# Attention ahead of two MoE layers: the maxima of the first six head pairs move to another PSUM pool

## The chip, the cores and the metric

The kernel runs on one core of one Trainium2 chip. The metric is the device time of one execution in microseconds (us). Before the change three runs took 1105.35, 1109.31 and 1111.76 us; the median is 1109.31 us.

## What is computed

Attention over 4 batches, 12 heads, 448 positions and 64 channels, then two MoE-like layers on 1792 tokens of width 768. Cut to what matters:

```python
q_n, k_n = rmsnorm(q, g_q), rmsnorm(k, g_k)
scores = scale * q_n @ k_n.T
scores = scores - max(scores, axis=-1)          # a maximum per query
attn = exp(scores); attn /= sum(attn) + 1e-9
x = (attn @ v)            # laid out as (1792, 768)
h = x @ w_in1; sm = softmax(h); x = layernorm(h * sm) * g_ln @ w_out1     # 768 -> 1024 -> 768
h = x @ w_in2; out = (h - tanh(h)) @ w_out2                               # 768 -> 2048 -> 768
```

The weights arrive as 64-bit floats and are converted on the chip; a product is made of three matmuls of a high and a low part (`three`, L189).

## The kernel before

**Pairs.** Two heads of one batch make a pair: 24 pairs, six to a batch (`HP = 6`). For a pair `p` the steps are:

- `load_qk`, `norm`: load and normalise q and k.
- `qk_trans` (L272): two **turns**, of k and of q. TensorE transposes into a PSUM tile `qkps`; ScalarE takes the high part and VectorE the low part, and DMAs copy both into the large tiles `K` and `Q` (`k<-wk`, `q<-wq`).
- `maxima` (L333): seven matmuls of 128 queries by 448 keys (`mps`); VectorE reduces each to a column of `nm` (L351, 0.6 us). The scores are only wanted for their maxima here.
- `spread` (L353): for each head `n` of the pair (`n = 2p`, `2p + 1`), `nm` is transposed (`nmps`), ScalarE writes the row `nt`, and a DMA of 2 KB puts it into a row of `Q` (`q<-nt`, L363). So the score matmuls subtract the maximum by themselves.
- `weights` (L365): the scores the other way round, in tiles `sps` of 128 keys by 448 queries, three to a head and one for the tails of both. A tile takes two matmuls: the first (z = 0) doesn't need the row of maxima, the second (z = 1) does (in pair 0: three, L380 to L382, and the fourth, L383). ScalarE makes the exponential `pf` (L395).
- `pv` (L399): `pf` times v into `pvps`; `pv_fin` and `x_norm` divide and store.

**PSUM.** Eight banks in three pools (L678 to L680): `ps_m` with three banks for the turns, the spread and the first MoE layer; `ps_x` with three for the maxima and for the scores; `ps_v` with two for `pvps`. Within a pool the tiles take the banks in turn, in the order of the program text: the fourth tile waits until the first has been read.

**Order.** The steps are written into a list with a slot (a head) and a step in it (a quarter of a slot), L452 to L476; the maxima of head `n` stand in slot `n`, its scores about two slots later. A scheduler then places the instructions of each engine's queue anew, by when operands and buffers come free in its own estimate; what stands below as the order is its result. The slots up to 15 are written ahead of everything else (L719): attention alone. They hold the maxima of pairs 0 to 7. After that `overlap` (L722) weaves the rest of the attention into the stages of the first MoE layer, whose first matmul is the first `hps` (L190). The second layer (`h2ps`, `ops`) comes last and fills TensorE alone.

**Streams.** While the first pairs run, the conversion of the first layer's weights has begun: loads of 512 KB (`raw<-in_moe_w_in_dram`, L115), work on ScalarE, VectorE and GpSimd (L135 to L161), and stores of 512 KB (`w_in<-w`, L164). All DMAs but three are issued from SP's queue, in its order.

Of the kernel before, what the change touches and what calls it, by code (L numbers as in the profile page):

```python
# [8 lines left out]
F32 = mybir.dt.float32  # L9
# [9 lines left out]
def kernel(  # L19
# [15 lines left out]
    B, H, S, D = q.shape  # L35
# [6 lines left out]
    HP = H // 2  # L42
# [169 lines left out]
    def qcols(t, o, p, i, z):  # L212

        c = (2 + i) * S + GAP if p == 0 else QO[i, z]
        return t[o, c:c + S]
# [117 lines left out]
    def maxima(p, c):  # L333


        if p not in nm_t:
            nm_t[p] = A["small"].tile([128, 7], F32, tag="nm", name="nm")
        ps = ps_x.tile([128, S], F32, tag="x", name="mps")
        i = c // 4
        r = slice(64 * i, 64 * i + 64)  # L340
        if c == 3:
            nc.tensor.matmul(ps, lhsT=qd[p % 2], rhs=w_t[p, 1][:, 0], start=True, stop=True)
        else:
            if p == 0:
                qh, kh = Q[0][r, 0:S], w_t[0, 1][r, 0]
            else:

                qh, kh = qcols(Q[p % NQ], slice(0, 128), p, i, 0), K[p % NQ][:, i, 0]
            f = 128 * c if i == 0 else 128 * (c - 4) + 64
            nc.tensor.matmul(ps, lhsT=qh[:, f:f + 128], rhs=kh, start=True, stop=True)  # L350
        nc.vector.tensor_reduce(out=nm_t[p][:, c:c + 1], in_=ps, axis=AX.X, op=ALU.max, negate=True)  # L351
# [100 lines left out]
    for p in range(NP):  # L452
        s = 2 * p
        at(s - 7, 0, load_qk, p)
        if 1 <= p <= NQ:
            at(s - 2 if p < NQ else 4, 1, fill, p % NQ)
            at(s - 2 if p < NQ else 4, 1, fill_q, p % NQ)
        at(s, 1, load_v, p)
        at(s - 3, 1, norm, p)
        at(s - 2, 2, qk_trans, p, 1)  # L460
        at(s - 1, 0, qk_trans, p, 0)
        for i in range(2):
            n, z = s + i, 4 * (s + i)
            for j, c in enumerate((3, 0, 1, 2) if i == 0 else (4, 5, 6)):
                step(z + j, maxima, p, c)
            step(z + 4, spread, n)
            for j in range(3):
                step(z + LAG + j, weights, n, j)
                step(z + LAG + 4 + j, pv, n, j)
        step(z + LAG + 3, weights, s + 1, 3)  # L470
        step(z + LAG + 4, pv_tails, s)
        step(z + LAG + 4, pv_fin, s)
        step(z + LAG + 6, pv_fin, s + 1)
        step(z + LAG + 8, x_norm, p)
# [203 lines left out]
    ps_m = ctx.enter_context(tc.tile_pool(name="ps_m", bufs=3, space=PSUM))  # L678
    ps_x = ep.enter_context(tc.tile_pool(name="ps_x", bufs=3, space=PSUM))
# [199 lines left out]
```

## Time and profile before

| | |
|---|---|
| median of three runs (lowest, highest) | 1109.31 us (1105.35, 1111.76) |
| span of the profiled execution, which is the time that the page gives of it | 1107.5 us |
| TensorE matmul busy | 1043.3 us, 94% |
| VectorE, ScalarE, GpSimd busy | 690.5, 493.1 and 236.4 us |
| first matmul; first matmul of an MoE layer (`hps`) | 11.28 us; 127.04 us |

A busy matmul row reaches from its start to its modelled end, so rows overlap, and a row that follows a slower one looks longer than its share of the engine. What one instruction takes from the engine is better read from the chain of waits, where each piece ends where the next begins.

### The profile page before, as it was taken

The page shows a single profiled execution, that of the slowest core. Times are in us where ns is not written, and L with a number is a line of the kernel's source. Part 1 is how long each engine was busy: PE and PEld are TensorE (multiplying, and loading weights), DVE is VectorE, ACT ScalarE, POOL GpSimd, SP SyncE. Part 2 cuts the span into 40 slices and gives each one's busy share as a digit, 9 for nine tenths or more (in the row PEclk, how much of TensorE's full clock was granted, in tenths as well). Part 3 has the DMA queues.
Part 4 walks back from the last instruction along what each step waited for, and adds up shares of the span by engine and source line. Part 5 has one row for each costly group of instructions (what it writes and reads, how often), then busy time and mean ns, then how long its engine had stood idle before and what let it go on. Part 6 is the DMA issues. An engine that isn't in the chain of part 4 may idle for free.

```text
span 1107.5 us, 15169 instructions
## 1 busy us (share of the span) xinstructions
PE 1043.3 (94%) x5348; PEld 864.2 (78%) x5348; DVE 690.5 (62%) x1311; ACT 493.1 (45%) x994; POOL 236.4 (21%) x204
## 2 busy tenths in 40 slices
PE   4989999989887899999999999999999999999998
PEld 2555566648664678778889989898999989898988
DVE  8766686787787453633684066475767666675444
ACT  4667776777677455555255154311212121212110
POOL 2511123121102110001420034242414141322000
PEclk9999999989988999999999999999999999999999
DMA  7987789866996987666786443021112111110004
GB/s 182 274 227 192 179 216 281 207 181 178 284 320 185 327 229 216 192 209 203 227 291 208 138 162 95 23 74 39 57 40 59 55 58 58 57 57 1 1 29 171
DMA packets 113743, 171.16 MB, mean 155 GB/s; under 512 B 31940, under 2 KB 79492, under 8 KB 113668
## 3 DMA queue, kind: packets, MB, share of 16 engines
q1 hardware_dynamic: 112368, 170.20, 52.8%
q8 instruction: 42, 0.69, 0.3%
q14 instruction: 33, 0.27, 0.1%
q10 hardware_dynamic: 1300, 0.01, 0.1%
HBM read 109.32 MB, written 29.10 MB: 125 GB/s over the span
## 4 chain that ended last, share of the span: by engine, by line
PE 72%; DMA 15%; DVE 6%; ACT 4%; issue 1%; SPq 1%; POOL 1%; ACTq 0%; DVEq 0%; POOLq 0%
PE pvps L409 9%; PE ops L191 7%; PE ops L192 7%; PE ops L190 7%; PE h2ps L191 7%; PE h2ps L192 7%; PE h2ps L190 7%; PE sps L386 4%; DMA raw<-in_moe_w_out_dram 3%; PE x2ps L190 3%; PE x2ps L191 3%; PE x2ps L192 3%; DMA q<-nt 2%; DMA raw<-in_moe_w_in_dram 2%; DMA w<-w_in 2%; PE mps L350 1%
## 5 line engine op out<-in xcount | busy, mean ns | idle before, releaser
L820 DVE TENSOR_TENSOR ob<-ops,ob 128x384 f32<-128x384 f32 x196 | 108.5, 554 | 104.1 <-PE ops L192 103.6
L161 POOL TENSOR_TENSOR w<-val,w 128x512 fp32r<-128x512 f32 x60 | 82.5, 1377 | 424.6 <-ACT w L160 397.0
L409 PE MATMUL pvps<-pf,va 128*128 128x448 f32 (+1 forms) x384 | 164.9, 598 | 0.9 <-ACT pf L395 0.9
L191 PE MATMUL ops<-w,gT 128*128 128x384 f32 x448 | 150.6, 336 | 0.0
L190 PE MATMUL ops<-w,gT 128*128 128x384 f32 x448 | 150.3, 336 | 0.0
L192 PE MATMUL ops<-w,gT 128*128 128x384 f32 x448 | 150.2, 335 | 0.0
L351 DVE TENSOR_REDUCE nm<-mps 128x1 f32<-128x448 f32 x168 | 102.6, 617 | 71.1 <-PE mps L350 61.2
L192 PE MATMUL h2ps<-x2s,w 128*128 128x512 f32 (+1 forms) x384 | 140.9, 367 | 0.0
L386 PE MATMUL sps<-q,k 128*128 128x448 f32 (+1 forms) x368 | 118.1, 415 | 24.2 <-DMA q<-nt 9.7
L191 PE MATMUL h2ps<-x2s,w 128*128 128x512 f32 (+1 forms) x384 | 140.9, 367 | 0.0
L190 PE MATMUL h2ps<-x2s,w 128*128 128x512 f32 (+1 forms) x384 | 140.5, 366 | 0.0
L797 ACT ACTIVATE th<-h2ps 128x512 f32<-128x512 f32 (+1 forms) x64 | 34.8, 544 | 182.5 <-PE h2ps L192 182.3
L386 PEld LDWEIGHTS sps<-q,k 128*128 128x128 f32 (+1 forms) x368 | 63.0, 186 | 60.2 <-ACT pf L395 17.6
L395 ACT ACTIVATE pf<-sps 128x448 f32<-128x448 f32 x167 | 88.3, 539 | 38.5 <-PE sps L386 32.5
L409 PEld LDWEIGHTS pvps<-pf,va 128*128 128x128 f32 (+1 forms) x384 | 63.4, 202 | 42.9 <-issue 35.6
L190 PE MATMUL hps<-w,xs 128*128 128x256 f32 (+1 forms) x276 | 90.6, 329 | 2.6 <-DMA w<-w_in 2.6
L266 POOL TENSOR_TENSOR qn<-qk,rr 112x512 f32<-112x512 f32 x44 | 49.0, 1135 | 195.8 <-DVE rr L247 74.7
L350 PE MATMUL mps<-k,q 128*128 128x448 f32 (+1 forms) x144 | 78.4, 553 | 11.1 <-ACT pf L395 3.3
L191 PEld LDWEIGHTS ops<-w,gT 128*128 128x128 f32 x448 | 84.2, 188 | 4.7
L190 PEld LDWEIGHTS ops<-w,gT 128*128 128x128 f32 x448 | 84.2, 188 | 4.4
L192 PE MATMUL hps<-w,xs 128*128 128x256 f32 (+1 forms) x276 | 85.9, 313 | 0.0
L191 PE MATMUL hps<-w,xs 128*128 128x256 f32 (+1 forms) x276 | 85.7, 311 | 0.0
(118 smaller groups left out, 2042.0 us busy)
## 6 DMA issues: line engine op xcount, KB each, us to landing
w<-w_out SPq DMA_DIRECT2D x48, 512.0 KB
raw<-in_moe_w_in_dram SPq DMA_DIRECT2D x36, 512.0 KB
raw<-in_moe_w_out_dram SPq DMA_DIRECT2D x36, 512.0 KB
w<-w_in SPq DMA_DIRECT2D x24, 512.0 KB
k<-wk SPq DMA_DIRECT2D x46, 224.0 KB
q<-wq SPq DMA_DIRECT2D x46, 224.0 KB
w_in<-w SPq DMA_DIRECT2D x12, 512.0 KB
w_out<-w SPq DMA_DIRECT2D x12, 512.0 KB
```

The lines of the kernel that those rows point to most:

```text
L161: nc.gpsimd.tensor_tensor(out=w[:, 1], in0=x, in1=w[:, 0].bitcast(F32), op=ALU.subtract)
L190: nc.tensor.matmul(ps, lhsT=a[0], rhs=w[0], start=first, stop=False)
L191: nc.tensor.matmul(ps, lhsT=a[0], rhs=w[1], start=False, stop=False)
L192: nc.tensor.matmul(ps, lhsT=a[1], rhs=w[0], start=False, stop=last)
L266: eng.tensor_tensor(out=qn[:, a].rearrange("p c h d -> p h c d"), in0=t[:, a], in1=rr[:, a].rearrange("p h (c o) -> p h c o", o=1).to_broa ...
L350: nc.tensor.matmul(ps, lhsT=qh[:, f:f + 128], rhs=kh, start=True, stop=True)
L351: nc.vector.tensor_reduce(out=nm_t[p][:, c:c + 1], in_=ps, axis=AX.X, op=ALU.max, negate=True)
L386: nc.tensor.matmul(o, lhsT=K[p % NQ][:, i, z, k0:k0 + m], rhs=qcols(Q[p % NQ], slice(0, 128), p, i, z), start=(z == 0), stop=(z == 1))
L395: nc.scalar.activation(out=x, in_=ps, func=AF.Exp)
L409: nc.tensor.matmul(pv_t[n], lhsT=w, rhs=pc_t.pop((n, j))[r], start=first, stop=last)
L797: nc.scalar.activation(out=th, in_=ps, func=AF.Tanh)
L820: nc.vector.tensor_tensor(out=o, in0=ps, in1=o, op=ALU.add)
```

## The change

The maxima of pairs 0 to 5 (`p < HP`) take their banks from `ps_m`, under its tag `"m"`; those of the other pairs stay in `ps_x`. The tile's shape and everything computed are the same.

```diff
-        ps = ps_x.tile([128, S], F32, tag="x", name="mps")
+        early = p < HP
+        ps = (ps_m if early else ps_x).tile([128, S], F32, tag="m" if early else "x", name="mps")
```

Line numbers behind it grow by one (L350 becomes L351). No instruction is added or left out. The scheduler makes another order of it, up to the first `hps`: on TensorE 315 instructions stand ahead of it in both, and of the 3739 last ones all stand alike.

The numbers in the names tell tiles apart. `mps_477` to `mps_598` are the maxima of pair 2, `nmps_480` is the spread of head 3, `nmps_546` that of head 4; `sps_463` to `sps_601` are the scores of pair 1 (heads 2 and 3), `sps_608`, `sps_630` and `sps_639` those of head 4.

**TensorE, from the spread of head 4 to the scores that need its row.** Before:

```order
L358 MATMUL nmps_546<-idf_63,nm_476 4x128
L386 MATMUL sps_551<-q1_158,k1_155 128x448 x2
L276 MATMUL qkps_557<-idf_63,qn_433 128x112 x4
L350 MATMUL mps_574<-k2_156,q2_159 128x448
L386 MATMUL sps_577<-q1_158,k1_155 128x448 x2
L350 MATMUL mps_598<-k2_156,q2_159 128x448
L386 MATMUL sps_601<-q1_158,k1_155 128x448 x2
L386 MATMUL sps_601<-q1_158,k1_155 64x448 x2
L386 MATMUL sps_608<-q2_159,k2_156 128x448 x2
```

Now, from the row behind the spread and the turn (the second matmul of `sps_608` stands two rows further on):

```order
L387 MATMUL sps_601<-q1_158,k1_155 128x448 x2
L387 MATMUL sps_601<-q1_158,k1_155 64x448 x2
L387 MATMUL sps_608<-q2_159,k2_156 128x448
L351 MATMUL mps_574<-k2_156,q2_159 128x448
L387 MATMUL sps_630<-q2_159,k2_156 128x448
L351 MATMUL mps_598<-k2_156,q2_159 128x448
L410 MATMUL pvps_534<-pf_606,va_352 128x448
L410 MATMUL pvps_614<-pf_606,va_352 128x448
L410 MATMUL pvps_614<-pf_532,va_352 128x448
L410 MATMUL pvps_614<-pf_554,va_352 128x448
L387 MATMUL sps_639<-q2_159,k2_156 128x448
L410 MATMUL pvps_614<-pf_580,va_352 128x448
```

The first matmuls of all three score tiles now run ahead, and five `pvps` stand between the spread and the second matmuls, which follow as three in a row.

**TensorE, behind the spread of head 3.** Before, the eleven rows from it on, up to the second tile of head 2; the scores of head 3 come six rows later:

```order
L358 MATMUL nmps_480<-idf_63,nm_326 4x128
L276 MATMUL qkps_514<-idf_63,qn_433 128x112 x4
L409 MATMUL pvps_469<-pf_460,va_246 128x448
L409 MATMUL pvps_469<-pf_384,va_246 128x448
L342 MATMUL mps_477<-wk_369,qd0_150 128x448
L409 MATMUL pvps_469<-pf_401,va_246 128x448
L409 MATMUL pvps_469<-pf_429,va_246 128x448
L386 MATMUL sps_463<-q1_158,k1_155 128x448
L409 MATMUL pvps_386<-pf_460,va_246 128x448
L386 MATMUL sps_485<-q1_158,k1_155 128x448 x2
L350 MATMUL mps_491<-k2_156,q2_159 128x448
```

Now, from the row behind it to the first matmul that needs the row of head 3 (the last):

```order
L351 MATMUL mps_491<-k2_156,q2_159 128x448
L351 MATMUL mps_511<-k2_156,q2_159 128x448
L387 MATMUL sps_529<-q1_158,k1_155 128x448
L410 MATMUL pvps_534<-pf_466,va_352 128x448
L276 MATMUL qkps_514<-idf_63,qn_433 128x112 x4
L387 MATMUL sps_551<-q1_158,k1_155 128x448
L410 MATMUL pvps_534<-pf_488,va_352 128x448
L351 MATMUL mps_526<-k2_156,q2_159 128x448
L387 MATMUL sps_577<-q1_158,k1_155 128x448
L410 MATMUL pvps_534<-pf_497,va_352 128x448
L351 MATMUL mps_543<-k2_156,q2_159 128x448
L387 MATMUL sps_529<-q1_158,k1_155 128x448
```

The spread of head 3 now stands behind all scores of head 2, and less work lies between it and the scores of head 3.

**SP's queue, around the row of head 3** (`nt_482`). Before:

```order
L115 DMA raw64_1435<-in_moe_w_in_dram 128x2x512
L363 DMA q1_158<-nt_482 1x4x128
L164 DMA w_in_3_1433<-w6_1424 128x1024
L316 DMA k0_154<-wk_519 64x448 x2
L315 DMA k0_154<-wk_519 64x896 x2
```

Now:

```order
L115 DMA raw64_1435<-in_moe_w_in_dram 128x2x512
L313 DMA q2_159<-wq_409 64x448 x2
L164 DMA w_in_3_1433<-w6_1424 128x1024
L232 DMA va_647<-in_v_dram 128x3x64 x2
L236 DMA va_647<-in_v_dram 128x1x64
L115 DMA raw64_1448<-in_moe_w_in_dram 128x2x512
L164 DMA w_in_4_1446<-w6_1437 128x1024
L364 DMA q1_158<-nt_482 1x4x128
```

A load and a store of 512 KB, which before stood directly ahead of the row of head 4, now stand directly ahead of the row of head 3.

## Rows read from the trace of the kernel before

**Rows 1.** Busy time by stretch (start:end, length, busy us by engine, PEclk, DMA share, GB/s):
```profile
11.00:127.00 116.00, 101.57 (x364) 59.55 (x365) 84.72 (x175) 80.56 (x175) 28.58 (x29) 0.97 0.87 222
...
274.00:330.00 56.00, 47.50 (x242) 35.57 (x241) 46.38 (x101) 39.83 (x96) 5.75 (x6) 0.91 1.02 301
...
600.00:1107.00 507.00, 504.10 (x2725) 464.55 (x2724) 291.79 (x482) 119.21 (x211) 120.19 (x80) 1.00 0.21 67
```
**Rows 2.** Timeline of TensorE: the first matmul, early scores, the first hps:
```profile
11.28 0.98 PE L276 MATMUL qkps<-idf,qn 112*128 112x112 f32 x4 [11.28 <-DVE nr L246]
...
21.90 0.38 PE L358 MATMUL nmps<-idf,nm 128*4 128x128 f32 x1 [1.52 <-DVE nm L351]
...
27.13 0.57 PE L381 MATMUL sps<-q,k 64*128 64x448 f32 x1
27.50 0.57 PE L382 MATMUL sps<-q,k 64*128 64x448 f32 x1
...
33.03 0.36 PE L381 MATMUL sps<-q,k 64*128 64x448 f32 x1
33.23 0.37 PE L382 MATMUL sps<-q,k 64*128 64x448 f32 x1
...
127.04 0.36 PE L190 MATMUL hps<-w,xs 128*128 128x256 f32 x1
```
**Rows 3.** Chain of waits, 53 to 64 us (start, length, what):
```profile
53.98 0.40 PE sps L386 x2
54.38 0.20 PE mps L350
54.58 0.75 PE pvps L409 x2
...
55.77 6.58 DMA q<-nt
...
63.07 0.11 PE nmps L358
63.18 0.55 PE qkps L276 x4
```
**Rows 4.** Waits of TensorE, 0 to 128 us (us in total, times, longest):
```profile
PE sps L386 <- DMA q<-nt: 2.7, 1, 2.7
PE mps L350 <- ACT pf L395: 2.4, 2, 1.3
...
PE sps L386 <- DVE nm L351: 1.2, 2, 1.0
```
**Rows 5.** Busy time by stretch, short ones (columns as in rows 1):
```profile
60.00:64.00 4.00, 1.60 (x9) 1.20 (x11) 1.41 (x3) 1.81 (x5) 0.00 (x0) 0.91 0.98 270
64.00:68.00 4.00, 4.00 (x10) 1.76 (x9) 2.72 (x9) 2.49 (x6) 0.00 (x0) 0.67 0.70 156
...
112.00:116.00 4.00, 2.31 (x10) 1.14 (x8) 3.04 (x6) 3.91 (x9) 0.00 (x0) 1.00 0.42 91
```
**Rows 6.** Chain of waits, other pieces (landings, and a spread four pairs after that of rows 3):
```profile
22.64 2.29 DMA q<-nt
...
107.54 4.52 DMA xr<-xd
...
118.17 0.11 PE nmps L358
...
219.59 2.98 DMA q<-nt
```
**Rows 7.** Timeline around 113 us, ScalarE's exponential and TensorE's wait for it:
```profile
113.30 0.52 ACT L395 ACTIVATE pf<-sps 128x448 f32<-128x448 f32 x1
113.88 0.47 PE L350 MATMUL mps<-k,q 128*128 128x448 f32 x1 [1.12 <-ACT pf L395]
```
**Rows 8.** Timeline of VectorE: the first turn of pair 1 and a maximum:
```profile
17.85 0.68 DVE L288 SCALAR_TENSOR_TENSOR wk<-qkps,gam,wk 128x448 fp32r<-128x448 f32 x1
...
21.23 0.61 DVE L351 TENSOR_REDUCE nm<-mps 128x1 f32<-128x448 f32 x1
```

## The prediction

> **What bounds the kernel now.** I read first the busy time by stretch [rows 1]. From 600 us to the end TensorE is busy 504.10 of 507 us at a granted clock of 1.00: the second layer is TensorE's alone, and the change does not reorder it. From 274 to 330 us the DMA share is 1.02, and TensorE idles 8.5 us. The change acts before all that, from the first matmul at 11.28 us to the first `hps` at 127.04 us [rows 2], a stretch of 115.8 us. So the whole question is when that first `hps` comes, and whether what is gained there is kept.
>
> How much of the 115.8 us does TensorE need? The chain of waits has the clean prices [rows 3]: two score matmuls 0.40 us, so 0.20 each; a maximum 0.20; one product with v, which is two passes, 0.75; a spread 0.11, with its load some 0.2; four transposes 0.55 behind an idle stretch, I take 0.5. By the order 315 matmuls stand ahead of the first `hps`: 54 maxima (10.8 us), 122 scores (24.4), 51 products with v (38.3), 72 transposes (9.0) and 15 spreads (3.0): 85.5 us. The stretch is 30 us longer. Part of that is a slow start: in pair 0 the step from L381 to L382 is 0.37 us at 27 us, and 0.20 us at 33 us [rows 2], as at the two levels of the clock (1.2 and 2.4 GHz), although the granted clock of the whole stretch reads 0.97 [rows 1]. Up to about 32 us TensorE did, in 20.7 us, what costs 7.6 us at the full clock (20 transposes, 8 maxima, 8 scores, 2 products, 2 spreads). From 32 us on it did the other 77.9 us in 95.0: 17.1 us of slack is all that a better order can work on there.
>
> The waits of that slack [rows 4]: one of 2.7 us for a row of maxima; 2.4 us of maxima that wait for exponentials and 1.2 us of scores that wait for reductions, which are the two kinds that shared banks alone make. The rest is short gaps and clock.
>
> **The change, part by part.** It adds and removes no instruction. Durations are those of the profiled execution, span 1107.5 us, 1.8 us below the median of the runs; the sum is made against 1107.5.
>
> *Shared banks.* The cross waits go: 1.2 us of scores behind reductions, and 2.4 us of maxima behind exponentials, 3.6 us at most [rows 4]. But one of the two waits of the second kind, 1.12 us at 113.88, comes from a ScalarE that was held by `xr`, a load of 4.52 us for the MoE [rows 6, 7]; the scores and products behind it need the same exponentials, so what ends late next is they. That load stays in ScalarE's queue. I count half: -1.8 us, between 0 and -3.6.
>
> *The wait for the row of head 4.* Before, between its spread and the matmul that needs it lie seven scores and the first of the next tile (1.6 us), two maxima (0.4) and a turn (0.5), about 2.6 us of TensorE; the DMA landed 6.58 us after its issue [rows 3], and TensorE waited 2.7 us [rows 4]. Behind the wait the granted clock is 0.67 from 64 to 68 us [rows 5], which costs another 0.33 x 4 = 1.3 us. Now the cover is a turn (0.5), seven scores (1.4), two maxima (0.4) and five products (3.75): 6.1 us. With the same landing the wait is all but gone: -4.0 us. At the other even heads the cover grows likewise, where the trace shows no wait to remove.
>
> *The row of head 3.* At the odd heads the cover shrinks. Before, from the spread of head 3 the program reaches the scores of head 3 after some 8 us of work; now after four maxima (0.8), three scores (0.6), three products (2.25) and a turn (0.5): 4.15 us. A row lands in 2.29 us where DMAs are few and 2.98 us in a later stage [rows 6], and 6.58 us behind 512 KB transfers [rows 3]. The order on SP puts just such a store and such a load ahead of this row now. So between nothing and 6.58 - 4.15 = 2.4 us of wait, and up to 1.3 us of clock behind it. I take half of the 2.4: +1.2 us. Queued behind that second score matmul are two more, and behind them the tail tile, the exponentials of the head and its products: all of TensorE's work of that moment, so a wait there is not hidden.
>
> *Scores that hold their banks.* With banks of their own the first matmuls of three score tiles run early and hold all three until the row is there. Then three second matmuls run 0.20 us apart, and for heads 5, 7 and 9 the tail tile comes next, in the bank of the first (for head 3 a spread and a turn stand between): it waits for an exponential, 0.36 us of matmul [rows 2] and 0.52 us [rows 7], with 0.6 us of cover, where ScalarE is free; an exponential more where it is not. Three times 0.3 to 0.8; I take the lower end, since ScalarE is busy 81 of 116 us [rows 1]: +1.0 us, up to 2.4.
>
> *Spreads of odd heads.* The last maximum is now followed by three scores and one maximum (0.8 us) ahead of the spread, where 1.2 us of scores stood. The reduction takes 0.61 us [rows 8] and starts some 0.36 us behind the matmul. Four times 0.2: +0.8 us, between 0 and 1.6.
>
> *The start.* The spread of head 0 now takes the bank of pair 1's first turn, and on VectorE that turn's low part (0.68 us at 17.85 [rows 8]) is moved behind the fourth maximum and three steps of the weight conversion. I read from the order of VectorE, with these durations, a spread at about 23.4 instead of 21.90 us [rows 2], 1.5 us later. Against this, nine score matmuls of pair 0 run in the gaps before it, at the slow clock (0.37 us each); by the end of the first product with v the new order has done seven scores more (2.6 us). I take 0 for the start, between -2 and +2.
>
> *Behind the first `hps`* the queue of TensorE is nearly the same instruction by instruction, and what is issued there is issued as buffers come free. A shift of the first `hps` moves it all. I count the shift in full.
>
> Sum: -1.8 - 4.0 + 1.2 + 1.0 + 0.8 + 0 = **-2.8 us**, a profile of 1104.7 us and a median of 1106.5 us. The bounds by themselves reach from -9.6 to +5.7 us (head 3 with its clock).
>
> **The rivals.**
>
> *The early stretch goes much nearer to TensorE's need.* The two streams of banks no longer lock step, and the short gaps go as well as the named waits. Of 17.1 us of slack, some 3.4 us is the two `xr` holds (TensorE is busy 2.31 of 4 us at 112 to 116 [rows 5], and once more like it); the rest could go down by two thirds. For it: more cover at even heads, score matmuls always at hand. Against: from the spread at 63.07 to the one at 118.17 four pairs take 55.1 us [rows 3, 6]; without the two holds and the 1.3 us of clock that is 12.6 us a pair, and by the prices above its own matmuls need 12.0 (seven maxima, sixteen scores, eight products, two turns, two spreads). At two thirds of 13.7 us, some -9, and with the 1 us that a quicker start may give, -10: a profile of 1097.5, a median of 1099 us.
>
> *Slower: the rows of odd heads come late.* One mechanism: the 4.15 us of cover. It decides where a row takes over some 4.2 us from spread to landing, which it does behind 512 KB transfers [rows 3] and does not behind small ones [rows 6]. If the rows of heads 3, 5 and 7 all land as late as 6.58 us, each costs 2.4 + 1.3 us: three times 3.7 = 11.1 in place of the 1.2 in the sum, so +7 us: 1116 us. For it: the DMA share is 0.98 at 60 to 64 us [rows 5]. Against: by SP's order the last load of the stretch is issued ahead of the row of head 5; from head 6 on nothing of that size stands in the way but `xr`.
>
> *Nothing is kept.* The gain comes, and the stage that is bound by DMAs at 274 to 330 us [rows 1] takes it back, if its loads do not move along: 1109.3 us. Against: they wait for buffers that TensorE frees.
>
> *The clock.* The waits at 58 to 62 us were followed by a stretch at 0.67, the one at 112 us of the same kind as now at the tail tiles by 1.00 [rows 5]. If each of ten heads' short waits brought such a stretch, 10 x 1.3 = 13 us would come on top: 1119.5 us. The rows speak against it, since 2.31 us of work in 4 left the clock at 1.00. The Trainium skill, "TensorE: Matmul & The Clock Gate", section "A second HAM failure mode: psum-queue depth-cycling", has a rule of this kind: a TensorE that cycles through PSUM banks and idles briefly between groups loses its clock again and again. By that rule the change would cost; the trace shows it for one place only.
>
> **How the numbers follow.** A measurement of this kernel tells about 0.5% from no change, 5.5 us. The forecast, a gain of 1 to 6 us, 0.45; the large gain 0.22; the late rows of odd heads 0.14; nothing kept 0.14; the clock 0.05. Faster by over 0.5% (below 1103.8): nine tenths of the large gain and a quarter of the forecast, 0.31, I say 0.32. Slower (above 1114.9): most of the late rows and the clock, 0.16. The same: 0.52. The range leaves out the clock, the worst of the late rows and the best of the large gain: 1097 to 1115 us.
>
> **What would show it.** Right: the first `hps` at about 124 us; no wait over 1 us for a row of maxima at 55 to 63 us and a granted clock of 1.00 behind it; no maxima waiting for exponentials before 127 us; small waits of scores for exponentials at the tail tiles; the stretch from the first `hps` to the end as long as before, 980.5 us. Wrong: waits of `sps` for `q<-nt` at several heads, which is the slower rival; a first `hps` before 120 us, which is the large gain; or a stretch behind the first `hps` that is longer by what was gained.

## The result, and the profile after

The changed kernel takes 1122.99 us (median of 6 runs, 1121.24 to 1127.65), the kernel before in the same comparison 1107.37 us: a ratio of 1.0145, 95% interval 1.0114 to 1.0176. It is slower by 13 to 19 us, outside the predicted range. The profiled execution of the changed kernel took 1122.3 us, span 1120.5. Its line numbers are higher by one from L338 on (L386 is now L387, L409 is L410).

TensorE's timeline shows where the time went (start, length, engine, line, operation; behind it the idle time before and what ended it):

```profile
22.63 0.37 PE L359 MATMUL nmps<-idf,nm 128*4 128x128 f32 x1 [1.02 <-DVE nm L352]
...
29.55 1.46 PE L384 MATMUL sps<-q,k 64*128 64x448 f32 x3 [2.99 <-DMA q<-nt]
...
39.52 0.57 PE L382 MATMUL sps<-q,k 64*128 64x448 f32 x1
39.89 0.57 PE L383 MATMUL sps<-q,k 64*128 64x448 f32 x1
40.39 1.86 PE L410 MATMUL pvps<-pf,va 128*128 128x448 f32 x2
...
49.21 3.65 PE L410 MATMUL pvps<-pf,va 64*128 64x448 f32 x4
51.98 1.25 PE L387 MATMUL sps<-q,k 128*128 128x448 f32 x1
53.03 2.85 PE L410 MATMUL pvps<-pf,va 128*128 128x448 f32 x6
...
140.57 0.36 PE L190 MATMUL hps<-w,xs 128*128 128x256 f32 x1
```

The first `hps` came at 127.04 us [rows 2] and comes at 140.57 now, 13.5 us later. From there to the end it is 1120.5 - 140.6 = 979.9 us against 980.5 before: all of the loss lies ahead of the first `hps`, and it is kept in full. In the rows above, L382 to L383 still takes 0.37 us at 39.5 us, where before the step was 0.20 us at 33 us [rows 2]. The first products with v at the full rate start behind 53 us: four of their matmuls take 3.65 us from 49.21, six take 2.85 us from 53.03.

So TensorE stayed at the lower of its two clock levels (1.2 in place of 2.4 GHz) until about 53.3 us; before, until about 32.3. How much is that? Here is the busy time by stretch of the changed kernel (columns as in [rows 1]): the stretches at the lower level ahead of the first `hps`, and the whole.

```profile
11.00:53.30 42.30, 35.41 (x85) 19.69 (x86) 29.81 (x66) 19.62 (x44) 10.79 (x10) 1.00 0.76 207
67.20:70.60 3.40, 3.40 (x11) 2.05 (x9) 3.37 (x7) 2.11 (x5) 0.00 (x0) 0.50 1.09 215
84.20:87.60 3.40, 3.18 (x11) 2.54 (x12) 0.00 (x0) 2.05 (x6) 0.00 (x0) 0.50 0.04 15
11.00:140.57 129.57, 109.97 (x366) 63.55 (x366) 87.94 (x174) 79.23 (x175) 28.54 (x29) 0.97 0.77 199
```

And the same of the kernel before, with the stretch behind its first rise (32.30 to 42.00):

```profile
11.00:32.30 21.30, 16.22 (x43) 9.11 (x43) 18.96 (x46) 12.39 (x29) 4.74 (x4) 1.00 0.88 227
32.30:42.00 9.70, 9.66 (x39) 5.62 (x38) 9.31 (x18) 6.53 (x13) 6.33 (x6) 1.00 1.06 295
49.60:53.00 3.40, 3.06 (x6) 2.11 (x7) 0.46 (x2) 3.33 (x7) 1.70 (x3) 0.50 1.06 332
63.30:66.70 3.40, 3.40 (x10) 1.43 (x8) 2.46 (x6) 2.43 (x6) 0.00 (x0) 0.50 0.63 153
11.00:127.04 116.04, 101.61 (x365) 59.59 (x366) 84.75 (x175) 80.60 (x175) 28.58 (x29) 0.97 0.87 222
```

Work at the lower level takes about twice its time (steps of 0.37 us for 0.20), so as an estimate half of the busy time there is lost: 42.0 / 2 = 21.0 us now, 22.7 / 2 = 11.3 us before, **9.7 us more**. Idle time is 129.57 - 109.97 = 19.6 us against 14.4, **5.2 us more**. Together 14.8; the busy time that is left (109.97 - 21.0 against 101.61 - 11.3) is 1.3 us less, which gives the 13.5. Most of it is lost by the first rise: up to 53.3 us TensorE did 35.41 / 2 = 17.7 us of work as the full level counts it; before, it had done as much (16.22 / 2 + 9.66) by 42.0 us, 11.3 us sooner. The granted clock column must be read with care: it is 1.00 for the first stretch of both kernels, where the steps say 0.50. Only the later stretches are on record in it.

The idle time is in the waits of TensorE from 0 to 128 us (us in total, times, longest):

```profile
PE sps L387 <- DMA q<-nt: 8.1, 5, 3.8
PE sps L384 <- DMA q<-nt: 3.0, 1, 3.0
...
PE sps L387 <- ACT pf L396: 2.0, 6, 0.7
...
PE mps L351 <- DVE nm L352: 0.2, 1, 0.2
```

Of the waits in [rows 4] the cross waits are gone: maxima no longer wait for exponentials, nor scores for reductions. In their place scores wait for rows of maxima (`q<-nt`): 3.0 us for head 0, and 8.1 us at heads 3, 5, 7, 9 and 11, all odd. The longest, head 5, in the chain of waits (start, length, what):

```profile
74.75 1.04 POOL qn L266
75.80 0.42 POOL va L230
76.22 1.24 SPq L220
77.50 0.46 SPq L221
78.05 5.22 DMA q<-nt
83.32 0.49 PE sps L387
```

Its spread ran at 74.40 us, but SP had the issues of the next pair's loads (L220, L221) first, and the first of them waited for GpSimd. The row was issued at 78.05 behind them and landed 5.2 us later, with 0.68 us of work for TensorE from 80 to 84 us.

### The profile page after: what moved, and what is told of

It reads as the page before. It is cut to its first block, busy times and chain, and to the rows that moved or that the text cites. A ratio compares the mean times of both kernels' runs of the same rounds, so it can differ in the third digit from the quotient of the medians.

```text
span 1120.5 us, 15181 instructions
## 1 busy us (share of the span) xinstructions
PE 1049.7 (94%) x5348; PEld 866.3 (77%) x5348; DVE 693.7 (62%) x1311; ACT 492.5 (44%) x994; POOL 236.6 (21%) x204
## 4 chain that ended last, share of the span: by engine, by line
PE 69%; DMA 17%; DVE 6%; ACT 5%; issue 2%; POOL 1%; SPq 1%; ACTq 0%; DVEq 0%; POOLq 0%
PE pvps L410 8%; PE ops L191 7%; PE ops L192 7%; PE ops L190 7%; PE h2ps L191 7%; PE h2ps L192 7%; PE h2ps L190 7%; PE sps L387 4%; DMA q<-nt 3%; PE x2ps L190 3%; PE x2ps L191 2%; PE x2ps L192 2%; DMA w<-w_in 2%; DMA raw<-in_moe_w_in_dram 2%; DMA w<-w_out 2%
## 5 line engine op out<-in xcount | busy, mean ns | idle before, releaser
L410 PE MATMUL pvps<-pf,va 128*128 128x448 f32 (+1 forms) x384 | 162.9, 591 | 0.5 <-ACT pf L396 0.5
L387 PE MATMUL sps<-q,k 128*128 128x448 f32 (+1 forms) x368 | 123.4, 425 | 27.7 <-DMA q<-nt 15.7
L387 PEld LDWEIGHTS sps<-q,k 128*128 128x128 f32 (+1 forms) x368 | 64.5, 188 | 63.1 <-DMA q<-nt 19.4
L410 PEld LDWEIGHTS pvps<-pf,va 128*128 128x128 f32 (+1 forms) x384 | 62.4, 199 | 44.4 <-issue 37.5
L138 POOL TENSOR_SCALAR val<-raw 128x512 f32<-128x512 f32 x48 | 79.3, 1653 | 29.6 <-DMA raw<-in_moe_w_in_dram 15.1
```

Of the source, the lines that this page charges most:

```text
L138: nc.gpsimd.tensor_scalar(out=fv, in0=fh, scalar1=2.0 ** -15, scalar2=None, op0=ALU.max)
L387: nc.tensor.matmul(o, lhsT=K[p % NQ][:, i, z, k0:k0 + m], rhs=qcols(Q[p % NQ], slice(0, 128), p, i, z), start=(z == 0), stop=(z == 1))
L410: nc.tensor.matmul(pv_t[n], lhsT=w, rhs=pc_t.pop((n, j))[r], start=first, stop=last)
```

## The experiments

T1 is the theory that the start costs most, through the clock; T2 that the rows of the odd heads do. All ratios are to the kernel before, run in the same comparison.

**Is it the change? A second profile.** The changed kernel, unaltered.

> The changed kernel once more, unaltered, for a second profile. If the 21 us that TensorE spent longer at its lower clock at the start (until 53 us, against 32 us before) belong to the change, the steps from L382 to L383 are again 0.37 us at 40 to 50 us, and the first `hps` comes at 139 to 142 us. If that was chance of the one execution (T2 then has to carry the loss), the clock rises before 40 us, and the time is below 1115 us or the loss sits in other waits.

One run, 1119.79 us; first `hps` at 140.4 us, steps of 0.37 us until about 54 us. The low start belongs to the change.

**Which pairs cost?** One line each:

```diff
-        early = p < HP
+        early = 1 <= p < HP    # e1_pairs1to5
+        early = p < 1          # e2_pair0
+        early = 3 <= p < HP    # f4_pairs3to5
+        early = 2 <= p < HP    # f5_pairs2to5
```

> The maxima of pair 0 go back to the shared banks, those of pairs 1 to 5 keep the banks of the turns. Theory T1 (of the 13.5 us that the first `hps` came later, some 9 to 11 were lost in pair 0: its spread and row came later and TensorE stayed at the low clock until 54 us): the step from L382 to L383 is 0.20 us from about 33 us on again, the first `hps` comes at 128 to 132 us, the time is 1108 to 1113 us. Theory T2 (the rows of the odd heads, head 5 above all, cost the time, and the start is only a shift that would be caught up): first `hps` at 137 to 141 us, 1118 to 1123 us.

> Only the maxima of pair 0 take the banks of the turns; those of pairs 1 to 5 stay in the shared banks. T1 (the start): the steps of pair 0 are 0.37 us until after 50 us, the first `hps` comes at 136 to 139 us and the time is 1116 to 1120 us. T2 (rows of odd heads): the start is late but caught up, first `hps` at 127 to 130 us, 1107 to 1111 us.

> The maxima of pairs 3 to 5 alone take the banks of the turns; pairs 0 to 2 stay in the shared banks, so that the start and the row of head 5 are as before. If the loss is all of the start and of the rows behind the last large loads (heads 1 to 5): 1103 to 1108 us, the same as before or faster by what the cross waits were (up to 3 us). If every odd head's row costs: three of them late by some 1 to 3 us with their clock, 1110 to 1115 us.

> The same for pairs 2 to 5: head 5, whose row cost most in the changed kernel (3.8 us of wait and a clock of 0.57 behind it), is in. T2: 3 to 6 us more than with pairs 3 to 5, 1109 to 1113 us. If head 5 was late only because the altered start had put its spread among the loads of the next pair: 1103 to 1108 us.

| pairs changed | median us | ratio, 95% interval | first `hps` in the profile | profiled run, us |
|---|---|---|---|---|
| 3 to 5 | 1106.01 | 0.9988, 0.9958 to 1.0019 | 125.7 | 1105.14 |
| 2 to 5 | 1111.99 | 1.0028, 0.9994 to 1.0062 | 127.8 | 1107.52 |
| 1 to 5 | 1116.23 | 1.0069, 1.0046 to 1.0092 | 129.6 | 1111.75 |
| 0 alone | 1111.99 | 1.0032, 1.0005 to 1.0060 | 132.4 | 1117.20 |
| 0 to 5 | 1122.99 | 1.0145, 1.0114 to 1.0176 | 140.6 | 1122.30 |

A profile is of one run, whose own time stands beside it; for pairs 2 to 5, 1 to 5 and pair 0 it lies 4 to 5 us off the median. The first matmul of the profiles in these tables comes between 9.5 and 11.3 us, which moves a first `hps` by as much.

The cost grows from 3 to 5 over 1 to 5 to 0 to 5; the 0.4% that pair 2 and pair 1 each add are within the intervals. Pairs 3 to 5 cost nothing that can be measured, although rows still come late there: scores wait 4.8 us for rows, 3.1 of it at heads 7 and 11 of the changed pairs, longest 1.9. Neither theory alone holds. T1 expected 1116 to 1120 us from pair 0 alone; it gives 1112, and its clock rises at about 34 us, to fall again from 42 to 52. Pairs 1 to 5 without pair 0 give 1116 us, 7.6 us of loss (0.69% of 1109), where T1 expected 1108 to 1113; the profile, of a run of 1111.75, does not show where the median loses it. Pair 0 and the others together cost 16 us, their sum is 11; by the intervals (13 to 19 us against 0.6 to 6.7 and 5.1 to 10.2) that need not be more than the sum.

What pair 0 does alone is seen in the reckoning that was made of the two kernels above, here of a run of 1117.20 us. Its stretches at the lower level, and the whole up to the first `hps`:

```profile
10.60:34.60 24.00, 19.98 (x49) 11.02 (x49) 20.35 (x48) 13.01 (x30) 7.04 (x6) 1.00 0.83 216
41.70:51.90 10.20, 10.06 (x17) 4.05 (x17) 6.20 (x13) 3.96 (x10) 6.41 (x6) 0.50 1.05 250
79.20:86.00 6.80, 6.03 (x15) 3.26 (x16) 1.80 (x7) 3.75 (x8) 1.78 (x2) 0.50 0.78 190
120.20:123.60 3.40, 3.34 (x11) 2.54 (x11) 3.05 (x6) 1.87 (x5) 0.00 (x0) 0.50 0.91 235
10.60:132.43 121.83, 109.29 (x366) 63.11 (x366) 85.80 (x174) 80.87 (x175) 27.51 (x29) 0.92 0.85 212
```

Half of 39.4 is 19.7 us lost to the lower level, nearly the 21.0 of the whole change, but in three later falls in place of a late first rise. Its idle time is 12.5 us, less than the 14.4 before. The profile of pairs 1 to 5 has 13.6 us lost to the lower level and 16.5 us idle. So in these profiles pair 0 brings most of the clock's loss, and more idle time comes with the later pairs.

**Is it idle time at the start?** Nine matmuls more in the wait for head 0's row, in the changed kernel, and behind the same maximum in the one before, where TensorE has no long wait:

```diff
             nc.tensor.matmul(ps, lhsT=qd[p % 2], rhs=w_t[p, 1][:, 0], start=True, stop=True)
+            if p == 1:
+                more = ps_v.tile([128, S], F32, tag="v", name="more")
+                for _ in range(9):
+                    nc.tensor.matmul(more, lhsT=qd[p % 2], rhs=w_t[p, 1][:, 0], start=True, stop=True)
```

> The changed kernel with nine more products of pair 1's first maximum into a tile that nothing reads; they stand where TensorE waited for the row of head 0 (24.84 to 29.55 us) and take 9 x 0.37 = 3.3 us there. T1 in the form 'idle time at the start keeps the clock low': the clock rises at about 32 to 36 us, the first `hps` comes some 8 to 10 us earlier, 1112 to 1116 us. If the idle time has nothing to do with it: 1122 to 1126 us.

> The kernel before with the same nine products behind pair 1's first maximum. TensorE waits there for nothing long, so they lie on the path: at the low clock 9 x 0.37 = 3.3 us, 1109 to 1112 us. If they raise the clock earlier than 32 us they pay for themselves: 1105 to 1108 us. That the changed kernel gains 10 us by them and this one nothing would show that the loss is the start's and not one that more work anywhere would mend.

The changed kernel gains: 1112.80 us, ratio 1.0048 (1.0023 to 1.0074), so added work takes 10 us off. The kernel before loses: 1110.39 us, 1.0035 (1.0010 to 1.0061). TensorE's timeline of the first:

```profile
25.37 3.54 PE L347 MATMUL more<-wk,qd 128*128 128x448 f32 x9
28.75 0.37 PE L343 MATMUL mps<-wk,qd 128*128 128x448 f32 x1
29.38 0.85 PE L388 MATMUL sps<-q,k 64*128 64x448 f32 x3 [0.27 <-DMA q<-nt]
...
32.45 0.71 PE L355 MATMUL mps<-k,q 128*128 128x448 f32 x1 [2.01 <-DMA q<-wq]
...
37.38 0.57 PE L386 MATMUL sps<-q,k 64*128 64x448 f32 x1
```

Behind the nine the scores step at 0.20 us. Then comes a wait of 2.01 us, and now that the clock has once been full, its fall is on record: 0.50 at 32 to 44 us.

```profile
32.00:36.00 4.00, 3.45 (x7) 1.96 (x7) 3.93 (x9) 2.44 (x7) 1.02 (x1) 0.50 1.00 327
36.00:40.00 4.00, 4.00 (x7) 1.33 (x5) 0.91 (x2) 0.67 (x1) 2.29 (x3) 0.50 0.95 345
40.00:44.00 4.00, 4.00 (x11) 2.44 (x11) 0.00 (x0) 0.00 (x0) 0.00 (x0) 0.50 0.35 109
```

From 36 to 44 us TensorE has no gap and yet stays at the lower level, as the changed kernel does. The first `hps` comes at 135.1 us. Between the two profiles lie 8.8 us (1120.5 and 1111.7): 5.4 ahead of the first `hps`, 3.3 behind it. The part behind is not clearly the fillers': in the second profile of the unaltered changed kernel that stretch is 977.6 us, here 976.6.

**A clock raised ahead of the first turn** (28 matmuls of the identity):

```diff
+    warm = ps_v.tile([128, 128], F32, tag="v", name="warm")
+    for _ in range(28):
+        nc.tensor.matmul(warm, lhsT=idf, rhs=idf, start=True, stop=True)
     attn_next()
```

> The changed kernel with 28 more matmuls of the identity on itself ahead of everything on TensorE; their result is read by nothing. T1 in its form 'the clock' (the work of pair 0 is slow because TensorE's clock is at its lower level, 1.2 GHz, until 54 us, and matmuls ahead of it would raise it): steps of 0.20 us in pair 0 from before 33 us, first `hps` 8 to 12 us earlier than in the changed kernel, 1111 to 1115 us. T1 in its form 'the row' (what is late is the row of head 0, the clock follows the gaps): steps of 0.37 us return in pair 0 as soon as TensorE waits for that row, and the time stays within 3 us of the changed kernel's 1123. T2: also within 3 us.

> The kernel before with the same 28 matmuls ahead of everything. If matmuls ahead of the first turn raise the clock for pair 0, the 20.7 us of slow start shrink by up to 4 us (first `hps` at 123 to 125, 1103 to 1105 us); if the clock falls again in the gaps between the first turns, nothing changes (1107 us), and if the added matmuls delay the first turn, it is 1 to 3 us longer.

The changed kernel: 1119.57 us, 1.0078 (1.0052 to 1.0104), less than the 1.0145 without them, but not the 1111 to 1115 us that were expected of a raised clock. The kernel before: 1120.57 us, 1.0117 (1.0087 to 1.0148), a loss that I had not expected. In both the clock was full for the first turn (four transposes in 0.55 us in the latter), and fell at 15.9 and 17.4 us in the gaps between the turns. It was back at 43.2 and 37.8 us, and in the latter low again from 41.2 to 48.1.

**What holds it low under gapless work?** The first score matmul of head 1's tiles three times more, in the same kernel again for a second profile, with the nine fillers besides, and last with operands that fill all 128 rows:

```diff
+                if n == 1:
+                    for _ in range(3):
+                        nc.tensor.matmul(o, lhsT=kh, rhs=qh, start=True, stop=True)
                 nc.tensor.matmul(o, lhsT=kh, rhs=qh, start=True, stop=False)
```

```diff
-                        nc.tensor.matmul(o, lhsT=kh, rhs=qh, start=True, stop=True)
+                        if m == 128:
+                            nc.tensor.matmul(o, lhsT=qd[1], rhs=w_t[1, 1][:, 0], start=True, stop=True)
+                        else:
+                            nc.tensor.matmul(o, lhsT=kh, rhs=qh, start=True, stop=True)
```

> The changed kernel with the first matmul of the score tiles of head 1 done three times more before it counts (9 full matmuls and, in the tail tile, 3 of 64 columns; the tile is begun anew behind them, so the sums stay as they are). They stand at 33 to 44 us, where TensorE is at the lower clock, and cost 9 x 0.37 + 3 x 0.37 = up to 4.4 us if nothing else changes: 1124 to 1128 us. If the sparse mix of that stretch (a group of three score matmuls, one product, small gaps at each change) holds the clock down, it rises before 45 us in place of 53 and the time is 1113 to 1120 us.

> The changed kernel with the repeats in the score tiles of head 1 once more, for a second profile: the first was of the slowest of its ten runs (1119.3 us, the others 1108.9 to 1115.3), and there the steps were 0.37 us until 59 us. If the usual run is faster because the clock rises earlier, a run of 1109 to 1115 us shows steps of 0.20 us before 50 us. If the steps are 0.37 us until about 59 us in such a run too, the gain of the repeats comes from elsewhere: fewer waits for rows, or fewer low stretches later.

> The same three repeats together with the nine products in the wait for the row of head 0. There the clock rose at about 29 us and fell at 32.0 until 45.6 us. If the density holds: it rises before 40 us, and the time is 1106 to 1111 us, below the 1112.8 us of the nine products alone. If not: 1114 to 1118 us.

> As the kernel with repeats (f2_dense), in the same places and as many, but the nine full repeats use all 128 rows of the array (the operands of pair 1's first maximum) where the repeats of the score tiles use 64. [...] If the 64 rows are what kept the clock low: steps of 0.20 us before 48 us, against 58.6 us in both profiles of the repeats with 64 rows, the first `hps` 4 to 9 us earlier (129 to 134 us), 1103 to 1109 us. If rows do not matter: the rise at 53 to 59 us again, the first `hps` at 137 to 139 us, 1110 to 1115 us.

| kernel | median us | ratio, 95% interval | clock full at | first `hps` | profiled run, us |
|---|---|---|---|---|---|
| repeats, 64 rows | 1112.09 | 1.0054, 1.0024 to 1.0084 | about 60 us | 138.2 | 1119.29 |
| the same, second profile | 1113.45 (one run) | | 58.6 us | 137.7 | 1113.45 |
| with the fillers | 1116.13 | 1.0068, 1.0041 to 1.0095 | 29, low again 32 to 49 | 136.2 | 1114.97 |
| repeats, 128 rows | 1115.28 | 1.0061, 1.0024 to 1.0098 | 35.4 us | 132.5 | 1112.49 |

The theory of the sparse mix fell: the time came down as it expected (by some 10 us), but with denser work of 64 rows the clock rose later, not earlier, and with the fillers it stayed low until 49 us. The two profiles of the 64-row repeats, of runs 6 us apart, agree in this. TensorE's timeline of the second profile, late:

```profile
51.75 0.57 PE L385 MATMUL sps<-q,k 64*64 64x448 f32 x1
52.13 0.57 PE L386 MATMUL sps<-q,k 64*64 64x448 f32 x1
...
54.83 3.65 PE L413 MATMUL pvps<-pf,va 64*128 64x448 f32 x4
57.59 1.26 PE L390 MATMUL sps<-q,k 128*128 128x448 f32 x1
58.65 2.75 PE L413 MATMUL pvps<-pf,va 128*128 128x448 f32 x6
```

The third, with 128 rows in the same places (`wk,qd`):

```profile
29.77 1.49 PE L384 MATMUL sps<-wk,qd 128*128 128x448 f32 x3 [0.57 <-ACT pf L402]
31.19 0.74 PE L387 MATMUL sps<-q,k 64*128 64x448 f32 x1
...
33.58 1.63 PE L351 MATMUL mps<-k,q 128*128 128x448 f32 x2
35.01 1.07 PE L384 MATMUL sps<-wk,qd 128*128 128x448 f32 x3
36.01 0.47 PE L387 MATMUL sps<-q,k 64*128 64x448 f32 x1
36.31 0.37 PE L388 MATMUL sps<-q,k 64*128 64x448 f32 x1
```

Three matmuls take 1.49 us at 29.77 and 1.07 at 35.01, and the scores behind step at 0.20. The clock is full 23 us earlier in this profile. The edit altered nothing but the operands of nine matmuls, 128 rows for 64 (and so their values too); the order is nearly the same. Of the 23 us, 1.4 are the whole program's earlier begin in this profile (first matmul at 9.53 for 10.96 us), and the wait ahead of the scores that need head 0's row was 0.7 us shorter (2.05 for 2.77). That the rows decide rests on this one profile. The scores of pair 0 use 64 rows (`64*128`). The changed order has them at 29 to 47 us in groups between single products; the order before had products and transposes close together at 28.4 to 32 us. The first `hps` came 5.2 and 5.7 us earlier than with 64 rows (1.4 and 1.7 of it by the earlier begin), as expected, although this kernel's clock fell again ahead of it (0.59 at 52 to 56, 0.71 at 64 to 68, 0.78 and 0.79 at 88 to 96 us), where the repeats of 64 rows show 1.00 from about 60 us on. But the time did not follow, 1115 us where 1103 to 1109 was expected. From the first `hps` to the end the profile takes 978.2 us, those with 64 rows 979.3 and 973.9: against the second of them most of the gain is lost there, against the first nothing. Where the median lost it no profile shows.

**Do the rows wait in SP's queue?** ScalarE issues them in its place, all of them or those of the first six pairs, also with the fillers:

```diff
-        nc.sync.dma_start(out=Q[p % NQ][o:o + 1, c:c + S + GAP].bitcast(F32), in_=nt.bitcast(F32))
+        (nc.scalar if p < HP else nc.sync).dma_start(out=Q[p % NQ][o:o + 1, c:c + S + GAP].bitcast(F32), in_=nt.bitcast(F32))
```

> The changed kernel with the DMA of the row of maxima issued by ScalarE, which makes the row, in place of SP. T2 (rows wait behind 512 KB loads on SP's queue): the row of head 0 lands in about 2.5 us where it took 5.9, that of head 5 is issued at once and lands in 2.3 to 3 us where it came 8.9 us behind its spread; the wait of 3.8 us at head 5 is gone and the clock behind it stays at 1.00; 4 to 8 us less, 1115 to 1119 us, and more if the clock of pair 0 rises earlier too. If the row waits for the DMA engines as such and not behind its queue: landing 5 to 6 us as before, 1121 to 1125 us.

> The kernel before with the same change of queue. If the rows wait behind the loads of SP's queue: the wait of 2.7 us for the row of head 4 and the low clock behind it go, 3 to 5 us less, 1103 to 1105 us. If they wait for the DMA engines: 1106 to 1110 us. If ScalarE's issues cost more than they save (16 issues ahead of exponentials): 1 to 3 us more.

> The changed kernel with the rows of the first six pairs alone issued by ScalarE, the later ones by SP as before. With ScalarE issuing all rows the first `hps` came 5.0 us earlier (135.6 against 140.6 us) and 8 us were lost behind it. If that loss comes from ScalarE's issues for the later pairs: first `hps` at 134 to 137 us, the stretch from there to the end 980 to 982 us, 1116 to 1120 us. If it comes from the early ones: 1121 to 1125 us. T2 (rows) is worth the difference to 1123; T1 (the clock until 53 us) stays as it is, with steps of 0.37 us at 40 to 47 us.

> The kernel before with the rows of the first six pairs issued by ScalarE. With all rows there the first `hps` came 1.3 us earlier (125.7), and 6 us were lost behind it. If the later pairs' issues were the loss: 1105 to 1107 us, the same as before or a little faster. If the early ones: 1110 to 1114 us.

> The changed kernel with both: the nine added products in the wait for the row of head 0, and the rows of the first six pairs issued by ScalarE. If T1 (the idle start, 10 us) and T2 (the rows, up to 5 us) are two separate costs, they add: first `hps` at 126 to 131 us, 1106 to 1111 us. If they are one (a late row matters because of the clock), no more than the filler gave: 1111 to 1114 us.

| kernel | median us | ratio, 95% interval | first `hps` | profiled run, us |
|---|---|---|---|---|
| changed, all rows | 1123.88 | 1.0150, 1.0117 to 1.0184 | 135.6 | 1125.36 |
| before, all rows | 1113.92 | 1.0053, 1.0029 to 1.0077 | 125.7 | 1114.25 |
| changed, first six pairs | 1116.98 | 1.0113, 1.0068 to 1.0158 | 139.3 | 1123.17 |
| before, first six pairs | 1107.87 | 1.0018, 0.9993 to 1.0042 | 124.1 | 1108.89 |
| changed, first six pairs, fillers | 1122.39 | 1.0154, 1.0111 to 1.0198 | 143.5 | 1126.21 |

For head 0 the queue is not the cause, and the waits at the odd heads do not go with it: 5.5 us with all rows from ScalarE and 8.6 with those of the first six pairs, for 8.1. With all rows there the first `hps` came earlier, but the stretch behind it took 988.0 and 986.7 us for 979.9 and 980.4. Head 0's row in the changed kernel, with SP as the issuer:

```profile
21.64 1.19 SPq L316 DMA_DIRECT2D k<-wk  x2
22.92 0.54 SPq L115 DMA_DIRECT2D raw<-in_moe_w_in_dram  x1
...
23.57 0.71 SPq L364 DMA_DIRECT2D q<-nt  x1
```

and from the chain of waits with ScalarE as the issuer of the first six pairs:

```profile
22.62 7.10 DMA q<-nt
```

There SP issued the same raw load at 22.04 us, so the row is behind it in time though in another queue, and it took 7.10 us. Behind the load in SP's queue it took 29.55 - 23.57 = 6.0, to the matmul that needs it. Before, it was issued at 22.64, ahead of the raw load at 23.45, and landed in 2.29 us [rows 6]. So for this row it goes by what was issued first, whichever the queue. How much of it is the raw load's is not shown: the two transfers of keys (`k<-wk`, L316) also stand just ahead of the row now, at 21.64 us, where before four of them had been issued from 17.16 to 19.7. Whether the changed kernel gains by the early rows is inconclusive, since its interval and that of the change overlap. The sum of both remedies failed outright, 1122.39 us where 1106 to 1111 was expected. In that profile the clock fell at 32.7 and stayed at the lower level until 60.0 us, 27 us; of the other profiles only the changed kernel with the 28 matmuls shows a fall as long (15.9 to 43.2 us).

No version beat the kernel before by more than the measurement can tell; pairs 3 to 5 alone comes nearest.

## Why the prediction was wrong

**The step that failed: the start.** The prediction had "I take 0 for the start, between -2 and +2". It measured some +11: that far TensorE was behind at 53.3 us, and (35.41 - 16.22) / 2 = 9.6 us of it is the lower clock level. The parts that I read were right in kind: the spread of head 0 was late, at 22.63 us for the 23.4 expected and 21.90 before, and the score matmuls ran ahead in the gaps. Two things were missing. First, I priced the late spread as 1.5 us of delay and did not ask on SP what would be issued in that time: the raw load and two transfers of keys went just ahead, and a row that lands in 2.29 us took 6. Second, the slow start was in the sum as a fixed cost that ends "about 32 us". What would end it, or put it off, was not asked. The trace and the runs show that it is a result of the order: 53 to 54 us in both profiles of the changed kernel, about 34 with pair 0 alone (and low again later), 35.4 with 128-row repeats.

**Second: the rows of odd heads.** "+1.2" in the sum for head 3 alone; the waits at the five odd heads sum to 8.1 us, less the 2.7 for head 4 that went. This is the mechanism of the slower rival (7 us, a chance of 0.14), except that head 5 and not head 3 was hit worst, and that it was joined to the start. Its own part cannot be taken from one run: pairs 3 to 5 alone have 3.1 us of such waits and lose nothing, pairs 2 to 5 between a gain of 1 and a loss of 7 us, pairs 1 to 5 lose 5 to 10.

**Right.** The cross waits went, and so did the wait for head 4's row; the 1.3 us of clock that I counted behind it did not, since both kernels have two low stretches there. The small waits of scores for exponentials came, 2.0 us up to 128 us and 2.6 up to the first `hps`, for 1.2 before; I had 1.0 and up to 2.4. The shift of the first `hps` was kept in full, 979.9 us from there to the end, 977.6 in the second profile; in the experiments that stretch lies between 971 and 988 us, so this holds for the pair of kernels and not for every edit. The sums hold but for two counts that move nothing: the matmuls listed ahead of the first `hps` add to 314, and between the spread of head 4 and the matmul that waited stood eight scores and one of the next tile, not seven and one.

**The clock rival** was half right, on the wrong rule. The Trainium skill, "TensorE: Matmul & The Clock Gate", section "A second HAM failure mode: psum-queue depth-cycling", has a TensorE that loses its clock again and again at short waits between groups. The trace does not agree for this change: after the first rise both kernels have two low stretches ahead of the first `hps`, 6.8 us in each kernel. What cost was the first rise, 21 us later.

**Open.** Why the clock first rises at 53 us with pair 0 and the later pairs together, and near 35 with either alone, and why a clock that rises early falls again in some kernels (fillers with rows from ScalarE, 128-row repeats) and holds in others. The runs show that it does, not what decides it. That the 64-row repeats gain 10 us by the median is explained by their profiles only in part: 2.4 to 2.9 us ahead of the first `hps`, 0.6 to 5.9 behind it.

## What to carry to other kernels

A slow start is not a constant: before costing a reordering near the first matmuls at zero, compare the step between like matmuls at both levels, and ask what the engine will do in the new order until the rate doubles. Where a small transfer moves by a microsecond, look on the issuing queues for the large one that now goes first. And try a change by stages: here the last three pairs cost nothing that could be measured, and the first three the rest.

## What the runs showed of the hardware

- The granted clock column reads 1.00 until the first fall is on record. In the changed kernel it shows 1.00 from 36 to 40 us with steps of 0.37 us; with the 28 matmuls ahead, which had raised the clock once, the same stretch with the same steps shows 0.50:

```profile
36.00:40.00 4.00, 4.00 (x8) 2.00 (x8) 0.00 (x0) 0.00 (x0) 1.46 (x2) 0.50 0.83 207
```

- TensorE stayed at the lower level through 21 us of work almost without a gap (31.8 to 53.3 us), in which matmuls of 64 rows alternated with products, maxima and transposes. Nine repeats of 64 rows left it there until 58.6 us, nine of 128 rows in the same places until 35.4 (one profile).
- A row of maxima took 2.29 us when issued ahead of a raw load, and 6.0 and 7.1 us when issued 0.6 us behind one and 2 us behind two transfers of keys, from the same queue and from another engine's.
- Work added can take time off: nine matmuls that nothing reads, 10 us.
